# Expert rows turned by VectorE through HBM, thresholds in PSUM, and a shorter step of the search

## The chip, the cores and the metric

The kernel runs on one core of a Trainium2 chip. A core has five engines, each with its own instruction queue that it works through in order: TensorE (PE in the profile; PEld is its weight load), VectorE (DVE), ScalarE (ACT), GpSimd (POOL) and SyncE (SP, here only an issuer of DMAs). DMAs move data between HBM and the on-chip memory SBUF; PE writes its products to PSUM, which DVE and ACT read. The metric is the device time of one execution in microseconds, the median of several runs.

## The reference

Sigmoid attention over 8 batches of 12 heads, 448 positions and head width 64, and then a mixture of experts on its 3584 rows of 768:

```python
def _moe_ref(x, w_gate, w1, w2):
    N, D = x.shape; E = w_gate.shape[1]; cap = N // E          # 3584, 768; 8; 448
    flat = (x @ w_gate).flatten()
    for idx in np.argsort(-flat):                              # best logit first
        tok, e = idx // E, idx % E
        if assigned[tok] >= 0 or counts[e] >= cap: continue
        assigned[tok] = e; counts[e] += 1
    for e in range(E):
        mask = assigned == e
        out[mask] = np.maximum(x[mask] @ w1[e], 0.0) @ w2[e]   # F = 1024
```

Each expert gets exactly 448 rows, and which rows is settled one expert after the other: the expert that fills up first is found by a search for the threshold at which 448 rows count for it, its rows are taken out, and the next is searched.

## The kernel before, in words

**Attention first.** The first third of the span is attention; its result is written to HBM as `xs`, one row of 768 per token. Within a row the 32-wide pieces lie in an order that suits DVE's 32x32 transposes.

**Then eight experts, one after the other on PE.** Every matmul of an expert is done as three products of split operands (high x high, high x low, low x high), so that an expert takes 288 products: 144 with w1 (L858, L860, L862: four groups of 36) and 144 with w2 (L895, L897, L899: three groups of 48). The rows stand on the moving side as `xh` and `xl`, [128, 6, 448], the high and low part of the turned rows; the weights come as units of 18 or 24 products, loaded by SP (L703, L707), split into `wh` by ACT (L714) and `wl` by POOL (L716; for the last two experts every second one by DVE). After each w1 group ACT writes `hh` and `yt` (L866, L869) and POOL subtracts them to `hl` (L870). After each w2 group DVE turns the result (turn_y, L792), SP stores it to HBM and reads it back as rows, and POOL scatters these to the output (L814).

**Rows of the next expert.** While expert kx runs on PE, the rows of kx + 1 are prepared, once the router has listed them (L376 writes the list): four gathers by POOL (L736) for blocks of 128, 128, 128 and 64 rows; ACT puts each block's pieces in order (`order`, L745); PE transposes it in two trios of 128-wide transposes (`xturn`, L762); ACT writes xh from PSUM (L765) and DVE xl = p - xh (L766).

**The router** works meanwhile, mostly on DVE. Of search k: `keys` (L164 to L171), `ends` (two PE transposes, L180), then nine steps of `grid_search`, each three counts (L187) and a small sum (L192 to L242) on DVE alone; then `prove`: PE turns the eight thresholds and sums the counts (L291, L292), DVE makes from them `few`, `kr`, `km` (L295 to L302), reads one value for a branch (L304), and picks the expert (`choose`, L312 to L327). PE then sums the picked marks (`place`, L335, L340), DVE makes one-hot tables (L362), and PE turns these into the list (L367, L374). `bank()` gives out the router's two PSUM banks in turn.

**The order is written out by hand** in the loop at the end. Each product of PE adds 189 to `clock` (107 in the first, cut group of expert 0). When clock passes `t_route`, the router's next piece is issued at that place in all queues, and t_route is set to clock plus what the piece yields (the T_ numbers) plus SLACK = 150. Row work and scatters are `chores` with due times; at most one goes in 1000 of clock (CHORE_NS). While the rows of an expert are being turned by PE, `hold` pauses the router:

```python
if t >= t_route and (not hold["left"] or t < hold["from"]):
    t_route = t + next(route, 0) + SLACK
```

These numbers set only places in the order; an engine still waits for what an instruction needs.

Of the kernel before, what the change touches and what calls it, by code (L numbers as in the profile page):

```python
# [7 lines left out]
F32 = mybir.dt.float32  # L8
F32R = mybir.dt.float32r
# [4 lines left out]
AF = mybir.ActivationFunctionType  # L14
OP = mybir.AluOpType
# [13 lines left out]
LATE_PER_STEP = 1  # L29
LATE_KEYS = 3  # L30
T_KEYS, T_KE, T_STEP, T_DVE, T_KAP, T_PICK, T_TOT, T_OH, T_BT = 3600, 2100, 2050, 2025, 500, 2600, 600, 3800, 600
T_GRID, T_PROVE, T_FOUND = (0, 2290, 2480, 2480, 2480, 2480, 2480), 3000, 9000
T_LATER = 1000
SLACK = 150
CHORE_NS = 1000
# [3 lines left out]
W_DVE = 84  # L39
Y_WAIT, Y_LATE = 5000, 26000  # L40
N_FIRST, N_FAST = 3, 9
PAD = 176
NONE = 1.0e30
FOUND = 0x43E00000
ORDER = 2500
HOLD_NS = 1000


class Consts:
# [7 lines left out]

def route_consts(nc, cp, K):

    K.G = cp.tile([128, 128], BF, name="c_G")  # L60
    ti = cp.tile([128, 128], I32, name="c_ti")
# [5 lines left out]
    nc.gpsimd.iota(t9, [[0, 1]], base=0, channel_multiplier=1)  # L67
    K.CN = cp.tile([128, 32], F32, name="c_CN")
    nc.gpsimd.memset(K.CN, 0.0)
# [61 lines left out]
class Router:  # L131
# [156 lines left out]
    def prove(self, k):  # L288
        nc, K, wk = self.nc, self.K, self.wk
        p = self.bank()  # L290
        nc.tensor.transpose(p[:, :128], self.base.to_broadcast([128, 128]), K.ident)  # L291
        nc.tensor.matmul(p[:, 128:256], self.cnt.to_broadcast([128, 128]), K.G, start=True, stop=True)  # L292
        tr, cr = (p[:, o:o + 128].rearrange("p (e c) -> p e c", c=16)[:, :, 0] for o in (0, 128))
        few, kr = wk.tile([128, 8], F32, name="r_few"), wk.tile([128, 8], F32, name="r_kr")
        nc.vector.tensor_scalar(few, cr, 447.5, NONE, OP.is_lt, OP.mult)  # L295
        nc.vector.tensor_tensor(kr, tr, few, OP.subtract)
        km = self.km = wk.tile([128, 1], F32, name="r_km")
        nc.vector.tensor_reduce(km, kr, AX.X, OP.max)
        nc.vector.tensor_tensor(few, cr, few, OP.add)
        nc.vector.scalar_tensor_tensor(few, kr, km, few, OP.is_equal, OP.mult)  # L300
        ok = wk.tile([128, 1], F32, name="r_ok")
        nc.vector.tensor_reduce(ok, few, AX.X, OP.add)  # L302
        found = nc.vector.value_load(ok[:1].bitcast(I32))
        with self.tc.If(found != FOUND, preferred_fallthrough_block=True, label=f"found{k}"):  # L304
            self.exact(kr)
            nc.vector.tensor_reduce(km, kr, AX.X, OP.max)
        self.choose(kr[:112], km[:112])
# [112 lines left out]
def moe_attention(tc, q, k, v, w_gate, w1, w2, out):  # L420
    nc = tc.nc
    B, H, S, D = q.shape
    DM = H * D
    E, _, F = w1.shape
    CP, NCH, NP, ND, NF = 112, S // 112, H // 2, DM // 128, F // 128
    G4 = 4
    PSUM = bass.MemoryType.PSUM
    with contextlib.ExitStack() as ctx:
        ctx.enter_context(tc.manual_schedule())
        cp = ctx.enter_context(tc.tile_pool(name="cp", bufs=1))  # L430
        rw = ctx.enter_context(tc.tile_pool(name="rw", bufs=2))
        dr = ctx.enter_context(tc.tile_pool(name="dr", bufs=1, space=bass.MemoryType.DRAM))
# [3 lines left out]
        ps_s = pctx.enter_context(tc.tile_pool(name="pa_s", bufs=3, space=PSUM))  # L436
        cp.tile([128, PAD], F32, name="pad")
        ld = actx.enter_context(tc.tile_pool(name="ld", bufs=2))
        wk = actx.enter_context(tc.tile_pool(name="wk", bufs=2))
        xa = actx.enter_context(tc.tile_pool(name="xa", bufs=1))  # L440

        xs = dr.tile([B * S, DM], F32, name="xs")
        ys = [dr.tile([S, DM], F32, name=f"ys{i}") for i in range(2)]
        K = Consts()
        K.ident = ident = cp.tile([128, 128], F32, name="ident")
        bias = cp.tile([128, 1], F32, name="bias")
# [115 lines left out]

        def scale():

            a = rw.tile([128, CP], F32, name="s_a", bufs=1)
            nc.vector.tensor_scalar(a.bitcast(I32), LE[:, 0].bitcast(I32), 0x7FFFFFFF, None, OP.bitwise_and)
            m = rw.tile([128, 2], F32, name="s_m", bufs=1)
            nc.vector.tensor_reduce(m[:, :1], a, AX.X, OP.max)
            yield
            p = ps_t.tile([128, 512], F32, name="tp")  # L570
            nc.tensor.transpose(p[:, :128], m[:, :1].to_broadcast([128, 128]), ident)
            nc.vector.tensor_reduce(m[:, 1:], p[:, :128], AX.X, OP.max)
            K.D = cp.tile([128, 1], F32, name="c_D")
            nc.vector.tensor_scalar(K.D.bitcast(I32), m[:, 1:].bitcast(I32), 0x7F800000, None, OP.bitwise_and)
            K.kw = cp.tile([128, N_FAST + 1, 3], F32, name="c_kw")
            nc.vector.tensor_scalar(K.kw, K.cw, K.D, None, OP.mult)
            K.base0 = cp.tile([128, 1], F32, name="c_base0")
            nc.vector.tensor_scalar(K.base0, K.D, -2.0, None, OP.mult)
            K.T0 = cp.tile([128, 3], F32, name="c_T0")
            nc.vector.tensor_scalar(K.T0, K.kw[:, 0], K.base0, None, OP.add)  # L580
            yield
# [31 lines left out]
        for i in range(NPR + 1):  # L613
# [26 lines left out]
            if old and old[1] == NP - 1:  # L640
                b = old[0]
# [42 lines left out]
        xp = ctx.enter_context(tc.tile_pool(name="xp", bufs=1))  # L684
# [40 lines left out]
                split_w(state["split"])  # L725
                state["split"] += 1

        xg, xq, XH = {}, {}, {}

        def blocks():  # L730
            for j in range(4):
                yield j, min(128, S - 128 * j)

        def gather(kx, j, n):
            t = xg[kx, j] = xp.tile([128, DM], F32, name="xr", bufs=XR_BUFS)
            nc.gpsimd.indirect_dma_start(out=t[:n], out_offset=None, in_=xs,  # L736
                                         in_offset=bass.IndirectOffsetOnAxis(ap=listed[kx][:n, j:j + 1], axis=0))

        def order(kx, j, n):

            xq[kx, j] = xp.tile([128, DM], F32, name="xq", bufs=2)
            to = xq[kx, j][:n].rearrange("p (r a j) -> p r a j", r=ND, j=32)
            of = xg[kx, j][:n].rearrange("p (a r j) -> p r a j", r=ND, j=32)
            if kx or j > 1:
                nc.scalar.copy(to, of)  # L745
            else:
                nc.scalar.copy(to[:, :3], of[:, :3])
                nc.vector.tensor_copy(to[:, 3:], of[:, 3:])
# [19 lines left out]
        scat, chores = [], []  # L768
# [152 lines left out]
        clock = [0.0]  # L921
# [23 lines left out]
        for kx in range(E):  # L945
            turned = kx + 1 == E
            start = clock[0]

            def prepare():
                t0 = clock[0]  # L950
                lag = max(ORDER + 5000, min(14000, start + 40000 - t0))
                for j, n in blocks():
                    if kx:
                        chores.append((t0 + 1500 * j, kx + 1, lambda j=j, n=n: gather(kx + 1, j, n)))
                    else:
                        gather(1, j, n)
                bl = list(blocks())
                hold.update({"from": t0 + lag - HOLD_NS, "left": 2 * len(bl)})

                def turn_x(j, n, hf):  # L960
                    xturn(kx + 1, j, n, hf, False)
                    hold["left"] -= 1
                chores.append((t0 + lag - ORDER, kx + 1, lambda: order(kx + 1, *bl[0])))
                for i, (j, n) in enumerate(bl):
                    def first(i=i, j=j, n=n):
                        turn_x(j, n, 0)
                        if i + 1 < len(bl):
                            order(kx + 1, *bl[i + 1])
                    chores.append((t0 + lag + 1500 * j, kx + 1, first))
                    chores.append((t0 + lag + 1500 * j, kx + 1, lambda j=j, n=n: turn_x(j, n, 1)))  # L970

            def flush(kx):
                for c in [c for c in chores if c[1] <= kx]:
                    chores.remove(c)
                    c[2]()

            for step, cost in enumerate(moe(kx)):
                clock[0] += cost
                t = clock[0]
                if kx == 0 and step == 35:  # L980
                    flush(0)
                if t >= t_route and (not hold["left"] or t < hold["from"]):
                    t_route = t + next(route, 0) + SLACK
                if not turned and kx + 1 in listed:
                    prepare()
                    turned = True
                if t >= t_chore:
                    c = next((c for c in chores if c[0] <= t), None)
                    if c:
                        chores.remove(c)  # L990
                        c[2]()
                        t_chore = t + CHORE_NS
            if not turned:
                while kx + 1 not in listed:
                    next(route)
                prepare()
            flush(kx + 1)
# [28 lines left out]
```

## Time and profile before

| | |
|---|---|
| median of 3 runs | 846.31 us (845.62 to 850.72) |
| the profiled execution | 850.65 us, span 848.9 us |
| mean granted clock | 0.975 |
| attention and first list | 0 to 309 us |
| experts 0 to 7 begin at | 309.1, 384.9, 450.2, 514.7, 579.9, 644.8, 716.7, 779.9 us |

In the rows that follow, a line of the order of time is: start in us, duration in us, engine, line, operation, output <- inputs, shapes, count, and in brackets the idle time before it with the instruction that ended it. Matmuls are pipelined, so that durations overlap and the distance of starts is what one costs. A line of groups is: line, engine, operation, names, shapes, count, then busy us in all and mean ns of one, then idle time before them with the releasers. A line of stretches is: from and to, length, busy us and count of PE, PEld, DVE, ACT and POOL, granted clock, DMA share, GB/s.

### The profile page before, as it was taken

What the parts mean: (1) busy time and instruction counts of PE and PEld (TensorE: products, weight loads), DVE (VectorE), ACT (ScalarE), POOL (GpSimd) and SP (SyncE); (2) the same over time, 40 slices, a digit from 0 to 9 for tenths busy, and PEclk for the clock granted to TensorE, in tenths of its full rate; (3) what the DMA queues carried; (4) which work ended last, traced back from release to release, by engine and by line L of the source; (5) the groups of instructions that cost most, each with busy time, mean ns of one, the idle gap of its engine ahead of it and who ended that gap; (6) DMA issues with size and microseconds to landing.
All of it is one profiled execution on the core that took longest, in us unless ns stands there. A gap on an engine that the chain in (4) does not pass through costs nothing. (4 is left out here: it accounts for less than half of the span.)

```text
span 848.9 us, 14982 instructions
## 1 busy us (share of the span) xinstructions
PE 800.0 (94%) x5150; PEld 616.0 (73%) x5150; DVE 502.6 (59%) x1426; ACT 409.7 (48%) x506; POOL 467.1 (55%) x446
## 2 busy tenths in 40 slices
PE   6999999999999259899999999999999998999996
PEld 3454544554544149889989999989889887889996
DVE  4677666667663768568568558568678563232150
ACT  6777777777775143333433433433433423541421
POOL 9744444444420035745865875874874883481661
PEclk9999999999999669999999999999999999999998
DMA  8887877777770262365566576575665664845733
GB/s 171 169 179 155 185 172 159 167 177 154 176 151 19 94 186 70 100 183 164 176 196 189 146 207 197 156 211 162 187 199 169 169 210 126 241 138 138 226 130 131
DMA packets 259705, 138.71 MB, mean 163 GB/s; under 512 B 187136, under 2 KB 248832, under 8 KB 259616
## 3 DMA queue, kind: packets, MB, share of 16 engines
q1 hardware_dynamic: 246880, 104.14, 48.1%
q0 software_dynamic: 10880, 33.28, 13.0%
q8 instruction: 41, 0.67, 0.3%
q10 hardware_dynamic: 1856, 0.23, 0.2%
q14 instruction: 48, 0.39, 0.2%
HBM read 105.02 MB, written 32.57 MB: 162 GB/s over the span
## 5 line engine op out<-in xcount | busy, mean ns | idle before, releaser
L716 POOL TENSOR_TENSOR wl<-wr,wh 128x768 fp32r<-128x768 f32 (+1 forms) x96 | 203.5, 2133 | 68.9 <-ACT wh L714 66.0
L504 ACT ACTIVATE at<-sc,bias 128x896 f32<-128x896 f32 x168 | 161.6, 1004 | 40.7 <-PE sc L514 23.3
L464 POOL DMA_DIRECT2D nkq<-in_q_dram x188 | 118.5, 643 | 113.3 <-DVE kqT L489 106.1
L895 PE MATMUL sc<-hh,wh 128*128 128x448 f32 (+2 forms) x400 | 148.5, 371 | 0.4 <-ACT yt L827 0.4
L897 PE MATMUL sc<-hl,wh 128*128 128x448 f32 (+2 forms) x400 | 146.6, 367 | 0.0
L899 PE MATMUL sc<-hh,wl 128*128 128x448 f32 (+2 forms) x400 | 146.6, 366 | 0.0
L714 ACT ACTIVATE wh<-wr 128x768 fp32r<-128x768 f32 (+1 forms) x112 | 101.7, 937 | 92.1 <-PE sc L897 67.6
L862 PE MATMUL sc<-xh,wl 128*128 128x448 f32 (+2 forms) x396 | 144.8, 366 | 0.0
L858 PE MATMUL sc<-xh,wh 128*128 128x448 f32 (+2 forms) x396 | 144.1, 364 | 0.2 <-ACT xh L765 0.2
L860 PE MATMUL sc<-xl,wh 128*128 128x448 f32 (+2 forms) x396 | 144.2, 364 | 0.0
L870 POOL TENSOR_TENSOR hl<-yt,hh 128x896 fp32r<-128x896 f32 x32 | 68.1, 2129 | 96.0 <-ACT yt L869 84.8
L538 PE MATMUL tp<-at,nv 128*64 128x448 f32 x576 | 118.8, 548 | 0.0
L866 ACT ACTIVATE hh<-sc 128x896 fp32r<-128x896 f32 x32 | 29.5, 921 | 142.1 <-PE sc L862 142.1
L498 DVE TENSOR_TENSOR kqL<-kqT,kqH 128x896 fp32r<-128x896 f32 (+1 forms) x49 | 52.5, 1073 | 56.6 <-ACT kqH L497 56.5
L895 PEld LDWEIGHTS sc<-hh,wh 128*128 128x128 f32 x400 | 78.3, 196 | 4.6 <-ACT yt L827 0.6
L897 PEld LDWEIGHTS sc<-hl,wh 128*128 128x128 f32 x400 | 78.3, 196 | 4.6 <-issue 0.9
L899 PEld LDWEIGHTS sc<-hh,wl 128*128 128x128 f32 x400 | 78.3, 196 | 3.8 <-issue 0.2
L860 PEld LDWEIGHTS sc<-xl,wh 128*128 128x128 f32 x396 | 75.6, 191 | 6.0 <-DVE xl L766 0.4
L538 PEld LDWEIGHTS tp<-at,nv 128*64 128x64 f32 x576 | 37.1, 136 | 59.1 <-issue 56.7
L858 PEld LDWEIGHTS sc<-xh,wh 128*128 128x128 f32 x396 | 75.7, 191 | 5.8 <-ACT xh L765 0.4
L862 PEld LDWEIGHTS sc<-xh,wl 128*128 128x128 f32 x396 | 75.6, 191 | 5.7
L736 POOL DMA_INDIRECT xr<-xs,r_idx x32 | 32.0, 1001 | 72.8 <-ACT wh L714 57.2
(187 smaller groups left out, 1115.7 us busy)
## 6 DMA issues: line engine op xcount, KB each, us to landing
wr<-in_moe_w_dram SPq DMA_DIRECT2D x64, 384.0 KB
wr<-in_moe_w_dram SPq DMA_DIRECT2D x48, 512.0 KB
nkq<-in_k_dram SPq DMA_DIRECT2D x192, 56.0 KB
nkq<-in_q_dram POOLq DMA_DIRECT2D x188, 56.0 KB, 2.9
ys<-yt SPq DMA_DIRECT2D x92, 112.0 KB
xs<-xz SPq DMA_DIRECT2D x28, 336.0 KB
nv<-in_v_dram SPq DMA_DIRECT2D x92, 96.0 KB
xr<-ys SPq DMA_DIRECT2D x21, 384.0 KB
```

The lines of the kernel that those rows point to most:

```text
L464: qn.dma_start(t[o:o + 32, n], rws[x])
L504: nc.scalar.activation(a, p[:, :, :S], AF.Sigmoid, bias=bias, scale=1 / math.sqrt(D))
L538: nc.tensor.matmul(p[j * 64:j * 64 + 64, :S], nat["v", b, g][:, h0 + j, c, :], AT[b, pr, c][:, j, :], start=(c == 0), stop=(c == 2 and pr ...
L714: nc.scalar.activation(hi, raw[u], AF.Copy)
L716: eng.tensor_tensor(lo, raw[u], hi.bitcast(F32), OP.subtract)
L858: nc.tensor.matmul(ph[:, f, lo:hi], wh[:, a, fs], xh[:, dd, lo:hi], start=st, stop=False)
L860: nc.tensor.matmul(ph[:, f, lo:hi], wh[:, a, fs], xl[:, dd, lo:hi], start=False, stop=False)
L862: nc.tensor.matmul(ph[:, f, lo:hi], wl[:, a, fs], xh[:, dd, lo:hi], start=False, stop=en)
L870: nc.gpsimd.tensor_tensor(h2, h0, h1.bitcast(F32), OP.subtract)
L895: nc.tensor.matmul(py[:, d2, :w], wh[:, a, dsl], h1, start=st, stop=False)
L897: nc.tensor.matmul(py[:, d2, :w], wh[:, a, dsl], h2, start=False, stop=False)
L899: nc.tensor.matmul(py[:, d2, :w], wl[:, a, dsl], h1, start=False, stop=(j == 1 and a == 3))
```

## The change

Four things are done together.

1. Rows of experts 5, 6 and 7 (X_DVE = 5) are turned by DVE: the four gathers come as one chore; SP writes each gathered block to an HBM buffer `xd` (put_rows) and reads it back in two parts, so laid out (get_blocks) that DVE's 32x32 transposes finish the turn. DVE writes the turned block over the gathered one, ACT copies it to xh and DVE subtracts to xl (xturn_dve). `hold` isn't set for these experts. The tile xq grows to two blocks, for which PAD shrinks and s_a takes a tile of r_KE's ring.
2. kr, the eight thresholds, stays in the PSUM bank of the proof.
3. The pauses between search steps become 2290 and 2200 in place of 2480.
4. T_PROVE goes from 3000 to 2800, T_FOUND from 9000 to 8400.

```diff
-T_GRID, T_PROVE, T_FOUND = (0, 2290, 2480, 2480, 2480, 2480, 2480), 3000, 9000
+T_GRID, T_PROVE, T_FOUND = (0, 2290, 2290, 2200, 2200, 2200, 2290), 2800, 8400
-PAD = 176
+PAD = 32
+X_DVE = 5
+X_AT, X_PUT, X_GET, X_TURN = 21000, 5500, 10700, 17500
...
-        few, kr = wk.tile([128, 8], F32, name="r_few"), wk.tile([128, 8], F32, name="r_kr")
+        few, kr = wk.tile([128, 8], F32, name="r_few"), p[:, 256:264]
...
+        xd = [dr.tile([S, DM], F32, name=f"xd{i}") for i in range(2)]
...
-            a = rw.tile([128, CP], F32, name="s_a", bufs=1)
+            a = rw.tile([128, 224], F32, name="r_KE")[:, :CP]
...
+        def put_rows(kx, j, n):
+            nc.sync.dma_start(xd[kx % 2][128 * j:128 * j + n], xg[kx, j][:n])
+
+        def get_blocks(kx, g):
+            z = xz[kx, g] = xp.tile([128, 2, DM], F32, name="xq", bufs=2).rearrange("p h (b c) -> p (h b) c", c=192)
+            nb = min(8, S // 32 - 8 * g)
+            v = xd[kx % 2][256 * g:256 * g + 32 * nb].rearrange("(b t) (a c) -> a t b c", t=32, a=4)
+            for a in range(4):
+                nc.sync.dma_start(z[32 * a:32 * a + 32, :nb], v[a])
+
+        def xturn_dve(kx, j, n):
+            if j == 0:
+                XH[kx] = (xp.tile([128, ND, S], F32R, name="xh", bufs=2),
+                          xp.tile([128, ND, S], F32R, name="xl", bufs=2))
+            xh, xl = (x[:, :, j * 128:j * 128 + n] for x in XH[kx])
+            x = xg[kx, j][:, :ND * n].rearrange("p (r t) -> p r t", r=ND)
+            nc.vector.transpose(x.rearrange("p r (b t) -> p b r t", t=32),
+                                xz[kx, j // 2][:, j % 2 * 4:j % 2 * 4 + n // 32].rearrange("p b (r i) -> p b r i", i=32))
+            nc.scalar.activation(xh, x, AF.Copy)
+            nc.vector.tensor_tensor(xl, x, xh.bitcast(F32), OP.subtract)
+
         def order(kx, j, n):
-            xq[kx, j] = xp.tile([128, DM], F32, name="xq", bufs=2)
+            if j % 2 == 0:
+                xq[kx] = xp.tile([128, 2, DM], F32, name="xq", bufs=2)
+            xq[kx, j] = xq[kx][:, j % 2]
...
             def prepare():
+                if kx + 1 >= X_DVE:
+                    t0 = max(clock[0], start + X_AT)
+                    todo = [(0, lambda: [gather(kx + 1, j, n) for j, n in blocks()])]
+                    todo += [(X_PUT + 1150 * j, lambda j=j, n=n: put_rows(kx + 1, j, n)) for j, n in blocks()]
+                    todo += [(X_GET + 2300 * g, lambda g=g: get_blocks(kx + 1, g)) for g in range(2)]
+                    todo += [(X_TURN + 1300 * j, lambda j=j, n=n: xturn_dve(kx + 1, j, n)) for j, n in blocks()]
+                    chores[:0] = [(t0 + t, kx + 1, f) for t, f in sorted(todo, key=lambda x: x[0])]
+                    return
```

More of the change, by code (lines that the diff above doesn't have):

```diff
@@ L726, in stream @@
                 state["split"] += 1
-        xg, xq, XH = {}, {}, {}
+        xg, xq, xz, XH = {}, {}, {}, {}
         def blocks():
```

## The prediction

> **What bounds the kernel now.** I read the page first, then the stretches between expert starts, then the order of time on PE, on DVE and on POOL.
>
> ```profile
> PE 800.0 (94%) x5150; PEld 616.0 (73%) x5150; DVE 502.6 (59%) x1426; ACT 409.7 (48%) x506; POOL 467.1 (55%) x446
> ...
> 579.90:644.80 64.90, 64.58 (x355) 58.34 (x354) 47.28 (x182) 25.23 (x34) 45.91 (x30) 1.00 0.62 183
> 644.80:716.70 71.90, 68.65 (x389) 60.27 (x388) 40.84 (x149) 25.23 (x34) 46.90 (x31) 0.98 0.58 167
> 716.70:779.90 63.20, 61.85 (x314) 57.01 (x313) 18.22 (x18) 25.30 (x35) 31.79 (x21) 1.00 0.61 186
> ```
>
> After a stretch come its length and the busy times of PE, PEld, DVE, ACT, POOL, then the granted clock. The three stretches are experts 4, 5 and 6. PE is busy nearly throughout, so what counts is what PE must do and where it stands. Expert 4 is the normal case (64.9 us). Expert 5 is 7 us longer at a clock of 0.98, and expert 6 is short of DVE work (18.2 us) because no search is left.
>
> ```profile
> 619.84 0.20 PE L374 MATMUL rt<-c_SEL,r_bt 128*64 128x4 f16 x2
> ...
> 636.46 0.37 PE L899 MATMUL sc<-hh,wl 128*128 128x448 f32 x1
> 636.67 0.49 PE L762 MATMUL tp<-ident,xq 128*128 128x128 f32 x3
> 636.91 0.46 PE L895 MATMUL sc<-hh,wh 128*128 128x448 f32 x1
> 637.21 0.36 PE L897 MATMUL sc<-hl,wh 128*128 128x448 f32 x1
> ...
> 639.78 0.37 PE L899 MATMUL sc<-hh,wl 128*128 128x448 f32 x1
> 640.08 0.40 PE L762 MATMUL tp<-ident,xq 64*128 64x64 f32 x3
> 640.41 0.48 PE L895 MATMUL sc<-hh,wh 128*128 128x448 f32 x1
> 640.73 0.37 PE L897 MATMUL sc<-hl,wh 128*128 128x448 f32 x1
> ...
> 645.20 0.36 PE L862 MATMUL sc<-xh,wl 128*128 128x448 f32 x1
> 659.18 0.37 PE L862 MATMUL sc<-xh,wl 128*128 128x448 f32 x1
> ```
>
> Between the last two rows lie 69 products, so a product takes 0.203 us. Three row transposes cost PE 637.21 - 636.46 less two products, 0.34 us; those of the short block cost 640.73 - 639.78 less two, 0.54 us.
>
> **What goes.** An expert has six trios of the first kind and two of the second: 6 x 0.34 + 2 x 0.54 = 3.1 us of PE, and they go for experts 5, 6 and 7. For 6 and 7 waits go with them:
>
> ```profile
> 700.07 0.37 PE L899 MATMUL sc<-hh,wl 128*128 128x448 f32 x1
> 702.63 0.55 PE L762 MATMUL tp<-ident,xq 128*128 128x128 f32 x3 [2.19 <-ACT xq L745]
> ...
> 703.90:707.30 3.40, 3.40 (x12) 2.69 (x10) 1.68 (x3) 1.39 (x3) 1.71 (x1) 0.51 0.42 109
> ...
> 734.76 0.55 PE L762 MATMUL tp<-ident,xq 128*128 128x128 f32 x3 [1.04 <-ACT xq L745]
> ...
> 351.61 0.37 PE L899 MATMUL sc<-hh,wl 128*128 128x448 f32 x1
> 354.25 0.19 PE L335 MATMUL rt<-c_ones,r_mk 112*64 112x1 bf16 x1 [2.28 <-DVE r_ei L327]
> ...
> 355.80:359.20 3.40, 3.40 (x10) 3.01 (x10) 2.91 (x8) 0.00 (x0) 1.02 (x1) 0.50 0.38 116
> ```
>
> Expert 6's rows arrive late: 2.2 us of wait at 702.63, which I round up to 3.1 for the trios behind it, and a stretch of 3.4 us at half clock. Ten products in 3.4 us (the last row) in place of 16.7 lose 1.4 us: 4.5 us for all of it. Expert 7's rows cost 1.0 us at 734.76, which I round up to 1.6 in the same way. Rows together: 3 x 3.1 + 4.5 + 1.6 = **15.4 us off**.
>
> The wait at 354.25 is that of search 1 for DVE. It has a cause that the change meets:
>
> ```profile
> 341.93 0.17 DVE L295 TENSOR_SCALAR r_few<-rt 128x8 f32<-128x8 f32 x1 [3.89 <-PE rt L292]
> 342.60 2.03 DVE L300 SCALAR_TENSOR_TENSOR r_few<-r_kr,r_km,r_few 128x8 f32<-128x8 f32 x1
> 349.96 2.25 DVE L312 SCALAR_TENSOR_TENSOR r_w<-r_kr,r_km,c_rank 112x8 f32<-112x8 f32 x1 [5.14 <-DVEq L304]
> ...
> 665.09 0.25 DVE L300 SCALAR_TENSOR_TENSOR r_few<-r_kr,r_km,r_few 128x8 f32<-128x8 f32 x1
> ...
> 812.94 7.91 DVE L716 TENSOR_TENSOR wl<-wr,wh 128x1024 fp32r<-128x1024 f32 x1 [5.93 <-ACT wh L714]
> 812.95 2.14 POOL L870 TENSOR_TENSOR hl<-yt,hh 128x896 fp32r<-128x896 f32 x1
> 815.04 4.73 POOL L716 TENSOR_TENSOR wl<-wr,wh 128x1024 fp32r<-128x1024 f32 x2
> ```
>
> L300 on eight columns takes 0.25 us or 2.03, and a DVE subtraction takes 7.91 us while POOL works through three of its own: a DVE instruction with its inputs in SBUF stands until POOL's is over. With kr in PSUM I take L300 and L312 at 0.25 each, 3.8 us less. From L295 to L335 DVE then needs 12.3 - 3.8 = 8.5 us; T_FOUND at 8400 leaves 46 products, 9.3 us (49 before). The wait of 2.3 us and its half clock (the last row above), 1.4, go: **3.7 off**. If kr in PSUM frees nothing, they stay.
>
> The Trainium skill ("SBUF — State Buffer", Who interferes with whom) states that a DVE instruction with two SBUF inputs and a GpSimd one that reads SBUF shut each other out for a whole instruction. The rows agree on the wait, though 7.91 outlasts three. It speaks for kr in PSUM and against the new row split (below).
>
> **What the search steps do.** A step in every 13 products in place of 14 (2290 + 150 and 2200 + 150 over 189 both round up to 13) and two shorter pauses bring each listing forward by 8 + 1 + 3 products. I walked through the written order: each product adds 189 (107 in the first, cut group), the router goes when its time is past, one chore in 1000. That walk puts the old index of expert 5 (L374) at product 183 of expert 4. The trace has it at 619.84, 39.9 us in, which is 183 products and 2.7 us for the router's small matmuls; so I trust the walk, and it puts the new one at product 142. PE's gain from that alone is nothing: products bound it. The cover is DVE's slack at the proof:
>
> ```profile
> 600.35 0.17 DVE L295 TENSOR_SCALAR r_few<-rt 128x8 f32<-128x8 f32 x1 [2.24 <-PE rt L292]
> ...
> 592.58 0.27 DVE L242 TENSOR_SCALAR r_base<-r_acc,c_kw,r_base 128x1 f32<-128x1 f32 x1
> 595.03 0.27 DVE L242 TENSOR_SCALAR r_base<-r_acc,c_kw,r_base 128x1 f32<-128x1 f32 x1
> ...
> 625.96 0.39 DVE L183 COPY r_KE<-rt 128x224 f32<-128x224 f32 x1 [0.30 <-issue]
> 628.39 0.45 DVE L187 TENSOR_SCALAR_CACHE_REDUCE r_junk<-r_KE,r_T 128x224 bf16<-128x224 f32 x1
> ```
>
> A step takes DVE 2.45 us; 13 products give it 2.64. From the last row turn to the proof there were 116 products and there will be 108, 1.6 us less out of a slack of 2.24. Searches 2 to 5 fit, barely.
>
> **Search 6 does not fit.** Rows turned by PE pause the router through `hold`; the new branch of prepare() returns before that. So search 6 runs from product 169 of expert 4 (ends) to product 273 (step 8), and the four row turns fall between its steps at 235, 242, 249 and 256, in DVE's one queue:
>
> ```profile
> L601 DVE STREAM_TRANSPOSE xz<-xt 128x896 f32<-128x896 f32 x21 | 23.1, 1102 | 0.0
> L498 DVE TENSOR_TENSOR kqL<-kqT,kqH 128x896 fp32r<-128x896 f32 x47 | 51.4, 1093 | 56.5 <-ACT kqH L497 56.5
> L714 ACT ACTIVATE wh<-wr 128x768 fp32r<-128x768 f32 x64 | 52.4, 844 | 48.6 <-PE sc L897 25.2 <-DMA wr<-in_moe_w_dram 19.4 <-POOL wl L716 2.4
> ```
>
> A turn is a transpose (1.10 x 768/896 = 0.94 us), the ACT copy (0.84) and the subtraction (0.94), each waiting for the one before and DVE idle through ACT's: 2.9 us with two handoffs, 1.6 for the short block, 10.3 in all. To the last subtraction DVE needs 2.9 (ends to the first count, by 625.96 and 628.39) + 7 steps x 2.45 + two y turns of 1.05 + 10.3 = 32.4 us. PE covers the 119 products to expert 5 in 24.2, and some 1.6 of a wait for POOL (below). Expert 5's first products need all of xh and xl: PE stands 32.4 - 25.8 = 6.6 us. Its proof of search 6 comes one product later, with two steps and a count still to do (5.4 us): 5.2 more. **About 11.8 us on**, and after it the clock: one to two stretches like those at 0.50, 1.4 us each; I take 2.0.
>
> The Trainium skill ("TensorE: Matmul & The Clock Gate", Part 1) has the clock halve after an idle window of about 3.4 us and return after a busy one. Here 2.6 us of waiting were enough (351.61 to 354.25). By the Trainium skill, too, one to two such windows follow.
>
> At experts 6 and 7 no search runs beside the turns (products 204 to 230), so 58 products, 11.8 us, are left before the rows are wanted. ACT loses four copies an expert and writes xh in four instructions in place of eight; it wasn't late there.
>
> **DMAs and POOL.** The four stores and eight loads of an expert go through SP, and wait there for gathers and stores; weight loads stand behind them. They are asked for three units ahead (11 to 15 us), and the rows have 10 us from store to turn, so I take nothing; bounds 0 and 4 us. The wider xq, PAD and the shared r_KE ring add no instruction. Gathers in a row hold POOL:
>
> ```profile
> 612.10 2.14 POOL L870 TENSOR_TENSOR hl<-yt,hh 128x896 fp32r<-128x896 f32 x1
> ...
> 714.48 0.97 POOL L736 DMA_INDIRECT xr<-xs,r_idx  x1 [0.16 <-issue]
> 718.26 1.42 POOL L736 DMA_INDIRECT xr<-xs,r_idx  x1 [0.30 <-issue]
> ```
>
> Four take 5.2 us from 714.48 on. In expert 4 they come at product 144, ahead of the fourth hl: that ends at 614.2 + 5.2 = 619.4, and PE asks for it at product 174, at 579.9 + 35.3 + 2.6 of router work = 617.8: 1.6 us late. In experts 5 and 6 they come at product 112 and I take 2 and 1.4 by the same count: **5 on**, between 0 and 8. Earlier listings also put expert 3's gathers behind scatters: 1 on, between 0 and 2.
>
> **Sum**, against the profiled execution (850.65 us, span 848.9, 4.3 above the median of 846.31): -15.4 - 3.7 + 11.8 + 2.0 + 5 + 1 = +0.7, or 851. I carry the difference to the median: **847 us, no change**. A measurement of this kernel tells about 1% from none, 8.5 us.
>
> **Rivals.** *Faster*: the pile-up at expert 5 stays below some 4 us, since it is the difference of 32 and 26 us and ACT's handoffs or the first count may be shorter; gathers hidden too. For it: experts 6 and 7 gain whole. Against it: DVE's row turns have no other place in its queue. 847 - 8 - 1.4 of clock - 4 = 833.5; chance 0.27. *Slower*: the subtraction of the rows has both inputs in SBUF, where L766 read PSUM. If POOL holds it as at 812.94, two of the twelve standing 5 to 7 us add some 11 where nothing covers them, at expert 5: 858. It decides once POOL queues two operations when DVE arrives; for it the 7.91, against it the gaps that 45.9 us of POOL in a stretch of 64.9 leave. Chance 0.22. By the Trainium skill's page "SBUF — State Buffer" (Who interferes with whom) a held instruction waits for one POOL operation, up to 2.4 us each. *kr in PSUM frees nothing*: 851, within the forecast's band; a fifth of its chance. Forecast 0.51.
>
> The range runs from the fast rival to the slow one, 833 to 858. Faster by over 1%: 0.27; within: 0.51; slower: 0.22.
>
> **What would show it.** No L762 for experts 5 to 7; expert 5's first product waiting for DVE's xl by 4 to 9 us and L291 just behind it by 3 to 7, clock 0.5 after; no wait at L335 in expert 0; L300 and L312 near 0.25 us; expert 6 near 60 us. The prediction is wrong if expert 5 starts without a wait, if a weight load is late behind SP's row loads, or if the new subtractions take over 2 us.

## The result: slower by 3.4%, and the profile after

The changed kernel takes 876.35 us (median of 4 runs, 874.75 to 878.66) against 846.7 us for the kernel before on the same chip: a ratio of 1.0344 [1.0314, 1.0373], some 30 us. The prediction said 847 with a range up to 858. Its profiled execution has a span of 875.6 us. In the changed kernel the rows' lines are L739 (gather), L743 (put_rows), L751 (get_blocks), L760, L762, L763 (the turn), L790 (row turns on PE); products are L886, L888, L890 (w1) and L923, L925, L927 (w2); L717 and L719 make wh and wl.

The head of the page after, and its row of the DMA queue that carries loads:

```profile
span 875.6 us, 14869 instructions
...
PE 800.9 (91%) x5078; PEld 613.1 (70%) x5078; DVE 501.2 (57%) x1426; ACT 399.6 (46%) x482; POOL 468.4 (53%) x446
...
q1 hardware_dynamic: 254176, 112.40, 57.6%
```

The first thing to see is what did *not* change. PE was busy for 800.0 us and is busy for 800.9: the row transposes that went (3 x 3.1 us by the prediction) are made up, it seems, by a mean clock of 0.962 in place of 0.975, and the added time is idle time of PE. Second, queue q1 takes 57.6% of the DMA engines. Before:

```profile
q1 hardware_dynamic: 246880, 104.14, 48.1%
```

Over the span, q1 has 3% more packets, 8% more bytes and 24% more time for them (the share times the span). So packets got longer, and the stretches say where. Of each kernel the same 50 us of attention (length, busy us of PE, PEld, DVE, ACT, POOL, clock, DMA share, GB/s), first before, then after:

```profile
50.00:100.00 50.00, 49.91 (x438) 25.12 (x436) 34.30 (x65) 36.80 (x41) 22.63 (x36) 1.00 0.80 175
```

```profile
50.00:100.00 50.00, 49.91 (x442) 25.80 (x444) 34.66 (x71) 38.14 (x42) 22.97 (x38) 1.00 0.98 175
```

The same 175 GB/s cost 0.98 of the DMA engines in place of 0.80, in code that no part of the change was meant to touch. In the stretch from 0 to 50 us, where PE waits for inputs, this costs time (before, then after):

```profile
0.00:50.00 50.00, 42.75 (x296) 22.07 (x298) 28.53 (x42) 36.01 (x41) 40.48 (x80) 1.00 0.86 169
```

```profile
0.00:50.00 50.00, 38.20 (x242) 19.11 (x246) 23.03 (x30) 30.03 (x34) 36.75 (x74) 0.97 1.15 142
```

PE did 242 matmuls there where it had done 296. Expert 0 begins at 316.5 us in place of 309.1.

The rest lies in the experts. Experts 2, 4, 5 and 6 after, and PE's main waits (the order of time on PE, of which only rows that begin with a wait are shown):

```profile
456.00:525.10 69.10, 66.02 (x353) 59.04 (x353) 42.12 (x190) 25.00 (x35) 45.98 (x30) 0.98 0.61 172
...
591.50:663.30 71.80, 61.96 (x330) 55.99 (x328) 53.44 (x212) 20.44 (x25) 42.44 (x28) 0.97 0.72 204
663.30:738.00 74.70, 68.10 (x365) 59.89 (x366) 31.05 (x86) 23.07 (x28) 46.17 (x31) 0.91 0.63 180
738.00:806.00 68.00, 62.16 (x289) 56.44 (x288) 20.79 (x19) 21.85 (x26) 34.14 (x24) 0.95 0.76 215
```

```profile
507.71 0.55 PE L790 MATMUL tp<-ident,xq 128*128 128x128 f32 x3 [3.08 <-ACT xq L773]
...
632.35 0.48 PE L925 MATMUL sc<-hl,wh 128*128 128x448 f32 x1 [2.14 <-POOL hl L898]
...
663.30 0.74 PE L886 MATMUL sc<-xh,wh 128*128 128x448 f32 x1 [7.70 <-ACT xh L762]
...
668.66 0.48 PE L293 MATMUL rt<-ident,r_base 128*128 128x128 f32 x1 [4.62 <-DVE r_base L244]
...
712.86 0.48 PE L925 MATMUL sc<-hl,wh 128*128 128x448 f32 x1 [1.81 <-POOL hl L898]
...
776.08 0.48 PE L925 MATMUL sc<-hl,wh 128*128 128x448 f32 x1 [1.90 <-POOL hl L898]
...
792.04 0.58 PE L923 MATMUL sc<-hh,wh 128*128 128x448 f32 x1 [2.47 <-ACT wh L717]
...
794.47 0.74 PE L927 MATMUL sc<-hh,wl 128*128 128x448 f32 x1 [1.47 <-POOL wl L719]
```

Each row names the next culprit: late gathers in expert 2 (507.71), the pile-up on DVE at expert 5 (663.30 and 668.66), gathers ahead of `hl` in experts 4, 5 and 6, and late weights in expert 6 (792.04, 794.47).

### The profile page after: what moved, and what is told of

Its sections match the earlier page's. It is cut to its first block, busy times and chain, and to the rows that moved or that the text cites. A ratio compares the mean times of both kernels' runs of the same rounds, so it can differ in the third digit from the quotient of the medians.

```text
span 875.6 us, 14869 instructions
## 1 busy us (share of the span) xinstructions
PE 800.9 (91%) x5078; PEld 613.1 (70%) x5078; DVE 501.2 (57%) x1426; ACT 399.6 (46%) x482; POOL 468.4 (53%) x446
## 3 DMA queue, kind: packets, MB, share of 16 engines
q1 hardware_dynamic: 254176, 112.40, 57.6%
q0 software_dynamic: 10880, 33.28, 13.5%
## 4 chain that ended last, share of the span: by engine, by line
PE 36%; DMA 9%; issue 7%; POOL 7%; DVE 5%; ACT 1%; SPq 1%; POOLq 0%; DVEq 0%; ACTq 0%
PE sc L886 7%; PE sc L888 7%; PE sc L890 7%; PE sc L927 4%; POOL wl L719 4%; PE sc L923 4%; PE sc L925 4%; DMA xr<-xs,r_idx 4%; DMA wr<-in_moe_w_dram 3%; DMA xd<-xr 1%; PE tp L790 1%; POOL out_dram L842 1%; DVE r_junk L189 1%; POOL hl L898 1%; DVE r_oh L364 1%
## 5 line engine op out<-in xcount | busy, mean ns | idle before, releaser
L719 POOL TENSOR_TENSOR wl<-wr,wh 128x768 fp32r<-128x768 f32 (+1 forms) x96 | 206.7, 2168 | 90.4 <-ACT wh L717 90.1
L886 PE MATMUL sc<-xh,wh 128*128 128x448 f32 (+2 forms) x396 | 146.2, 369 | 7.9 <-ACT xh L762 7.7
L717 ACT ACTIVATE wh<-wr 128x768 fp32r<-128x768 f32 (+1 forms) x112 | 101.2, 935 | 113.7 <-DMA wr<-in_moe_w_dram 69.9
L925 PE MATMUL sc<-hl,wh 128*128 128x448 f32 (+2 forms) x400 | 146.4, 366 | 5.9 <-POOL hl L898 5.9
L927 PE MATMUL sc<-hh,wl 128*128 128x448 f32 (+2 forms) x400 | 148.5, 371 | 1.6 <-POOL wl L719 1.6
L923 PE MATMUL sc<-hh,wh 128*128 128x448 f32 (+2 forms) x400 | 146.9, 367 | 2.9 <-ACT wh L717 2.5
L888 PE MATMUL sc<-xl,wh 128*128 128x448 f32 (+2 forms) x396 | 145.9, 368 | 0.0
L890 PE MATMUL sc<-xh,wl 128*128 128x448 f32 (+2 forms) x396 | 145.2, 367 | 0.0
L886 PEld LDWEIGHTS sc<-xh,wh 128*128 128x128 f32 x396 | 75.9, 192 | 15.5 <-ACT xh L762 8.1
L925 PEld LDWEIGHTS sc<-hl,wh 128*128 128x128 f32 x400 | 78.9, 197 | 11.0 <-POOL hl L898 7.0
L923 PEld LDWEIGHTS sc<-hh,wh 128*128 128x128 f32 x400 | 78.9, 197 | 7.3 <-ACT wh L717 2.8
L927 PEld LDWEIGHTS sc<-hh,wl 128*128 128x128 f32 x400 | 78.9, 197 | 6.6 <-POOL wl L719 2.6
L888 PEld LDWEIGHTS sc<-xl,wh 128*128 128x128 f32 x396 | 75.9, 192 | 6.7 <-DVE xl L794 0.4
L890 PEld LDWEIGHTS sc<-xh,wl 128*128 128x128 f32 x396 | 75.9, 192 | 6.4
L517 PE MATMUL sc<-kqH 64*128 64x448 f32 x288 | 59.8, 412 | 10.5 <-ACT kqH L500 10.5
```

Source lines behind the costliest of these rows:

```text
L717: nc.scalar.activation(hi, raw[u], AF.Copy)
L719: eng.tensor_tensor(lo, raw[u], hi.bitcast(F32), OP.subtract)
L886: nc.tensor.matmul(ph[:, f, lo:hi], wh[:, a, fs], xh[:, dd, lo:hi], start=st, stop=False)
L888: nc.tensor.matmul(ph[:, f, lo:hi], wh[:, a, fs], xl[:, dd, lo:hi], start=False, stop=False)
L890: nc.tensor.matmul(ph[:, f, lo:hi], wl[:, a, fs], xh[:, dd, lo:hi], start=False, stop=en)
L923: nc.tensor.matmul(py[:, d2, :w], wh[:, a, dsl], h1, start=st, stop=False)
```

## The experiments

Twelve runs. The kernel before was timed beside each; its median was 848.2 to 848.5 us in all three sets. In what follows "PAD" is a filler tile: the tiles of attention are allocated behind it.

### Where the tiles lie: PAD alone, and PAD put right

The change makes three things ahead of attention's tiles smaller: PAD by 144 floats (576 bytes a partition), s_a, which moves into another ring (448), and the two buffers of r_kr (64). Attention's tiles begin 1088 bytes lower. The first run takes the kernel before and shrinks PAD alone (576 bytes); the second takes the changed kernel and gives 64 bytes back, so that the shift is 1024.

```diff
 # the kernel before
-PAD = 176
+PAD = 32
```

> The kernel before with PAD = 32 in place of 176 and nothing else: all SBUF tiles behind the pad stand 576 bytes lower, no instruction changes. Theory A (place in SBUF): the changed kernel's extra 7 us in the attention stage, where the changed code does not run, come from where the tiles stand (576 is 64 more than a multiple of 128), which makes short DMA packets slower; then this run is slower by 5 to 20 us (852 to 867), its attention stage ends some 7 us later, and the 256-byte packets average about 24 ns instead of 18. Theory B (place in HBM, or more traffic): the two new buffers xd are the cause; then this run is 846 as before.

```diff
 # the changed kernel
-PAD = 32
+PAD = 48
```

> The changed kernel with PAD = 48 in place of 32: tiles 64 bytes higher, which gives the attention pools the same place modulo 128 (and 512) as in the kernel before. Theory A: packets are fast again and the run comes near the sum of the prediction, 847 to 855, with the attention stage ending near 304 us in place of 311. Theory B: 876 as the changed kernel.

PAD alone makes the kernel before slower, 858.38 us, ratio 1.0121 [1.0089, 1.0154]. Sixteen floats of filler make the changed kernel faster, 867.01 us, 1.0209 [1.0183, 1.0234] against 1.0344. The stretch shown above, of the changed kernel with PAD 48:

```profile
50.00:100.00 50.00, 49.91 (x442) 25.41 (x438) 34.20 (x69) 37.14 (x40) 22.56 (x36) 1.00 0.79 172
```

The share is back at 0.79. Packet by packet (mean time in the records of the DMA engines, 100 to 150 us):

| packet | before | after | after, PAD 48 | before, PAD 32 |
|---|---|---|---|---|
| 128 bytes | 13 ns | 15 ns | 13 ns | 15 ns |
| 256 bytes | 18 ns | 25 ns | 18 ns | 25 ns |

Packets of 768 bytes, by their number the stores of xs out of SBUF, went the same way (50 to 100 us): 47 ns before, 57 after, 48 with PAD 48, 57 in the kernel before with PAD 32. So some 10 us of the 30 come from an edit that adds no instruction: short packets into and out of tiles that stand 64 bytes off. The shifts tried were 64, 576 and 1088 bytes (slow) and 0 and 1024 (not slow), 64 and 0 in the runs with kr in PSUM below; which multiple counts is not told apart by these.

### What is left: the pile-up at expert 5

With PAD 48 the lengths of the experts, from first product to first product (the last to the end of the span), against before:

| expert | 0 | 1 | 2 | 3 | 4 | 5 | 6 | 7 |
|---|---|---|---|---|---|---|---|---|
| before | 75.8 | 65.3 | 64.5 | 65.2 | 64.9 | 71.9 | 63.2 | 69.0 |
| after, PAD 48 | 73.3 | 66.6 | 68.9 | 66.0 | 71.8 | 74.4 | 68.1 | 68.9 |
| difference | -2.5 | +1.3 | +4.4 | +0.8 | +6.9 | +2.5 | +4.9 | -0.1 |

Two runs tested the pile-up: one stops the router (search 6) while DVE turns expert 5's rows, the other leaves expert 5's rows on PE.

```diff
+                    hold.update({"from": t0 + X_TURN - HOLD_NS, "left": 4})
...
-todo += [(X_TURN + 1300 * j, lambda j=j, n=n: xturn_dve(kx + 1, j, n)) for j, n in blocks()]
+todo += [(X_TURN + 1300 * j, lambda j=j, n=n: turn(j, n)) for j, n in blocks()]   # xturn_dve, then hold["left"] -= 1
```

> As the run with PAD = 48, and the router paused through hold from 1000 ahead of the first row turn by VectorE to the last one, as rows turned by TensorE pause it. Theory C (search 6 and the row turns of expert 5 fight for VectorE, 11.8 us and a half clock): 10 to 14 us faster than the PAD = 48 run, and expert 5's first product waits 0 to 3 us in place of 8, the proof behind it not at all. Rival D (what holds expert 5's first product is the rows' way through HBM, with late loads): at most 4 us faster than the PAD = 48 run.

```diff
-X_DVE = 5
+X_DVE = 6
```

> As the run with PAD = 48, but X_DVE = 6: expert 5's rows are turned by TensorE as before. Theory C: 8 to 13 us faster than the PAD = 48 run (the pile-up goes, 3.1 us of transposes come back, one gather in a row less on the list). Rival D: within 4 us of it. If also theory A holds, the run is near 836 to 842 and beats the kernel before.

Stopping the router gave 864.31 us, 1.0183 [1.016, 1.0207]: 2.7 us better, far less than expected. PE's waits with it:

```profile
651.99 0.74 PE L886 MATMUL sc<-xh,wh 128*128 128x448 f32 x1 [3.18 <-ACT xh L762]
...
663.24 0.32 PE L293 MATMUL rt<-ident,r_base 128*128 128x128 f32 x1 [3.07 <-DVE r_base L244]
```

Both waits shrank and neither went: search 6 now comes later and PE waits for its proof all the same. In neither of the two orders tried does DVE get through its work in time. Leaving expert 5 on PE gave 852.98 us, 1.0059 [1.0042, 1.0076], 14.0 us better; expert 4 is back at 64.6 us and PE has no gap at expert 5's start. That shows DVE's turn of expert 5's rows as one cause, at 14 us, a little above what had been expected. The price is that of all that goes with these rows: the two waits and their half clock, the gathers ahead of `hl` in expert 4 (a wait of 2.1 us) and the rows' DMAs, less the 3.1 us of transposes that come back.

### kr in PSUM alone, the search numbers alone

```diff
 # the kernel before
-few, kr = wk.tile([128, 8], F32, name="r_few"), wk.tile([128, 8], F32, name="r_kr")
+few, kr = wk.tile([128, 8], F32, name="r_few"), p[:, 256:264]
```

> The kernel before with kr kept in the PSUM bank of the proof and nothing else (one SBUF tile of the ring goes, so tiles behind it may move by 64 bytes). The theory of the prediction: L300 and L312 fall to about 0.25 us, the wait at L335 in expert 0 (2.3 us and a half clock) goes, 3 to 4 us faster. Rival: kr in PSUM frees nothing, within 1 us of before. If the packets of 256 bytes are long again (24 ns), the place of the tiles has moved, and the attention stage must be taken out of the comparison.

```diff
 # the kernel before
-T_GRID, T_PROVE, T_FOUND = (0, 2290, 2480, 2480, 2480, 2480, 2480), 3000, 9000
+T_GRID, T_PROVE, T_FOUND = (0, 2290, 2290, 2200, 2200, 2200, 2290), 2800, 8400
```

> The kernel before with the four numbers of the search alone changed (steps every 13 products, shorter pauses). The prediction's step: nothing from it but 1 us from expert 3's gathers behind scatters, so 847 to 850 against 848.5. Theory E (earlier listings cost what the changed kernel lost in experts 1 to 3, 6.5 us by the starts of its experts): 3 to 7 us slower, with a wait of about 3 us at a row turn in expert 2.

kr alone gave 853.91 us, 1.0073 [1.0046, 1.0101]: slower, since leaving out r_kr moves the tiles by 64 bytes and the packets are long again (the DMA share of 50 to 100 us is 1.01). Expert 0 is nevertheless 72.8 us in place of 75.8. So a run with PAD put right was needed:

```diff
 # the kernel before, kr in PSUM
-PAD = 176
+PAD = 192
```

> The kernel before with kr in PSUM and PAD = 192, which gives back the 64 bytes that the missing kr tile moved the attention pools by. If the place of the tiles alone made the kr run slow (theory A): packets of 256 bytes at 18 ns again, attention ending near 304 us, and the 3.0 us that expert 0 gained there stay: 844 to 846 against 848.4, faster than the kernel before by 2 to 4 us. If kr in PSUM has another cost: 849 or more.

It gave 845.92 us, 0.9961 [0.9939, 0.9982], the one version that beat the kernel before, by 0.4%. Packets of 256 bytes take 18 ns again, where kr alone had 24. Its L300 (instances, min/median/max ns, first and last start), and that of before:

```profile
L300 DVE SCALAR_TENSOR_TENSOR r_few<-rt,r_km,r_few x7: 224/225/227, 289.1 to 664.6; 128x8 f32<-128x8 f32 x7
```

```profile
L300 DVE SCALAR_TENSOR_TENSOR r_few<-r_kr,r_km,r_few x7: 229/444/2107, 288.6 to 665.1; 128x8 f32<-128x8 f32 x7
```

With one operand in PSUM the instruction takes 224 to 227 ns in all seven searches; with three operands in SBUF it took up to 2107.

The four search numbers alone cost 6.5 us: 854.86, 1.009 [1.0066, 1.0114]. Two of PE's waits in that run:

```profile
354.77 0.19 PE L335 MATMUL rt<-c_ones,r_mk 112*64 112x1 bf16 x1 [3.07 <-DVE r_ei L327]
...
501.39 0.55 PE L762 MATMUL tp<-ident,xq 128*128 128x128 f32 x3 [1.83 <-ACT xq L745]
```

The first is the wait that kr in PSUM takes away; the second, late rows in expert 2, is the one that stands at 507.71 in the changed kernel.

### The rows of experts 6 and 7: SP's queue

With X_DVE = 6, expert 6 was still 67.2 us where before had 63.2. Where SP stood in the changed kernel (its waits: us in all, times, longest), and its queue in expert 5:

```profile
SPq L743 <- DMA xr<-xs,r_idx: 48.4, 12, 13.5
```

```profile
692.11 0.37 SPq L710 DMA_DIRECT2D wr<-in_moe_w_dram  x1
705.97 0.34 SPq L743 DMA_DIRECT2D xd<-xr  x1
706.57 0.37 SPq L710 DMA_DIRECT2D wr<-in_moe_w_dram  x1
```

SP takes the store of the first block, whose gather hasn't landed, and stands 13.5 us; the weight load behind it goes out at 706.57. ACT sees it (its waits, and two of them in its order of time):

```profile
ACT wh L717 <- DMA wr<-in_moe_w_dram: 69.9, 12, 17.8
```

```profile
714.24 1.06 ACT L717 ACTIVATE wh<-wr 128x1024 fp32r<-128x1024 f32 x1 [6.79 <-DMA wr<-in_moe_w_dram]
...
790.93 1.06 ACT L717 ACTIVATE wh<-wr 128x1024 fp32r<-128x1024 f32 x1 [10.07 <-DMA wr<-in_moe_w_dram]
```

Before, ACT waited 19.4 us in all for weights, 17.6 of them once at the start; after, 69.9. The wait of 10.07 us is the one that PE meets at 792.04. Two runs moved the stores 6 us later, with everything behind them, the second with the gathers apart again:

```diff
 # after, PAD 48, X_DVE 6
-X_AT, X_PUT, X_GET, X_TURN = 21000, 5500, 10700, 17500
+X_AT, X_PUT, X_GET, X_TURN = 21000, 11500, 17500, 24500
```

> PAD = 48, X_DVE = 6, and the rows' stores 6000 later (X_PUT 11500), loads and turns 6800 and 7000 later. Theory F (SP stands in front of put_rows until the gathers have landed, 12 us at its longest, and the weight loads behind it come late: the 8 us that expert 6 lost against the prediction): SP's wait at put_rows falls from 17 us to under 5, PE's waits for wh and wl in expert 6 (2.4 and 1.9 us) go, 4 to 8 us faster than the run with X_DVE = 6 (853), so 845 to 849. Rival G (the memory traffic itself is what makes loads late): the same waits stay, within 2 us of 853.

```diff
 # the run above
-todo = [(0, lambda: [gather(kx + 1, j, n) for j, n in blocks()])]
+todo = [(1500 * j, lambda j=j, n=n: gather(kx + 1, j, n)) for j, n in blocks()]
```

> As the run before it, and the four gathers of an expert 1500 apart in place of one chore. The prediction's step (gathers in a row hold POOL 5.2 us, so that the fourth hl comes 2 us late in each expert): the two waits of 2.4 us at unit 9 of experts 5 and 6 go, 3 to 5 us faster than with gathers in a row. Rival: POOL is short anyway, waits stay, within 1.5 us.

They gave 855.54 us, 1.0082 [1.006, 1.0104], and 856.39, 1.0092 [1.0072, 1.0112]: no better than 852.98. SP's wait has to be read with care here. The sums of the view are, with X_DVE = 6 and then with late stores:

```profile
SPq L743 <- DMA xr<-xs,r_idx: 17.3, 5, 12.1
```

```profile
SPq L743 <- DMA xr<-xs,r_idx: 19.2, 7, 5.6
```

They leave out three of the eight stores in the first run and one in the second. In SP's order of time, with X_DVE = 6, SP issues nothing between 670.10 and the first store of expert 6's rows:

```profile
660.41 9.69 SPq L710 DMA_DIRECT2D wr<-in_moe_w_dram  x4
683.67 2.21 SPq L743 DMA_DIRECT2D xd<-xr  x2
```

Counted so over all eight stores, SP stood 32.8 us ahead of them, and 19.5 with late stores (longest 13.6 and 5.7). The waits of PE for wh and wl in expert 6 (2.07 and 1.32 us) went with it, as expected; but PE now stands for the rows at the start of experts 6 and 7:

```profile
716.03 0.51 PE L886 MATMUL sc<-xh,wh 128*128 128x448 f32 x1 [2.13 <-ACT xh L762]
...
783.11 0.47 PE L886 MATMUL sc<-xh,wh 128*128 128x448 f32 x1 [1.82 <-ACT xh L762]
```

With the gathers apart the first of these is 4.52 us. That run also tests what gathers in a row cost: in expert 5, where an `hl` now goes between the second gather and the third, PE's wait for it (2.00 us) is gone; in expert 6 POOL still works through the four gathers without a break, and the wait stays (2.86 and 2.85 us).

The last set asks the same of expert 7 alone, with the old search numbers: X_DVE = 7; the same with late stores; and the same with stores and loads of the rows issued by GpSimd.

```diff
 # after, PAD 48
-T_GRID, T_PROVE, T_FOUND = (0, 2290, 2290, 2200, 2200, 2200, 2290), 2800, 8400
+T_GRID, T_PROVE, T_FOUND = (0, 2290, 2480, 2480, 2480, 2480, 2480), 3000, 9000
-X_DVE = 5
+X_DVE = 7
```

> The changed kernel with PAD = 48, the old numbers of the search, and X_DVE = 7: only expert 7's rows go through HBM and VectorE, during expert 6, where no search runs. Theory H (row traffic and its waits stand in front of the weight loads in SP's queue): expert 6 takes 67 to 69 us in place of 63.2, as in the changed kernel, and the run is 3 to 6 us slower than the run with kr and PAD = 192. The prediction's step (a row turn without a search beside it saves 4.7 us and costs 1.4): 3 us faster than that run.

```diff
 # the run above
-X_AT, X_PUT, X_GET, X_TURN = 21000, 5500, 10700, 17500
+X_AT, X_PUT, X_GET, X_TURN = 21000, 11500, 17500, 24500
```

> As the run before it with stores 6000, loads 6800 and turns 7000 later; the pair of the next run. Theory H: the waits move from unit 10 towards the start of expert 7, time within 2 us of the run before it.

```diff
 # the run above
-            nc.sync.dma_start(xd[kx % 2][128 * j:128 * j + n], xg[kx, j][:n])
+            nc.gpsimd.dma_start(xd[kx % 2][128 * j:128 * j + n], xg[kx, j][:n])
...
-                nc.sync.dma_start(z[32 * a:32 * a + 32, :nb], v[a])
+                nc.gpsimd.dma_start(z[32 * a:32 * a + 32, :nb], v[a])
```

> As the run before it, but put_rows and get_blocks are issued by GpSimd, so that SP's queue carries neither them nor their waits. Theory H in its first form (SP's order): weight loads land in time again, ACT's waits for wr in expert 6 (9 us each with rows on SP) fall under 5, and the run is 3 to 6 us faster than the run before it. Rival (the DMA engines' time: eight loads of 768-byte packets take 5 us of all sixteen, whoever issues them): ACT's waits for wr stay, within 1.5 us. GpSimd's own cost: eight to twelve issues of 0.6 to 1 us, at a time when it stands idle.

| run | us | ratio | SP's wait at L743, us (longest) | ACT's wait for weights, us (times) | expert 6, us |
|---|---|---|---|---|---|
| X_DVE 7 | 850.92 | 1.0026 [1.0006, 1.0045] | 16.5 (11.5) | 45.2 (8) | 67.7 |
| stores late | 848.67 | 0.9994 [0.9968, 1.0019] | 6.7 (4.3) | 37.8 (6) | 63.7 |
| by GpSimd | 857.01 | 1.0098 [1.0066, 1.013] | (not on SP) | 18.3 (3) | 70.5 |

The first two rows ask it with one expert's rows alone. SP's wait fell, and with it went the waits of PE for weights; with X_DVE 7 these were

```profile
764.65 0.48 PE L923 MATMUL sc<-hh,wh 128*128 128x448 f32 x1 [2.39 <-ACT wh L717]
...
767.09 0.74 PE L927 MATMUL sc<-hh,wl 128*128 128x448 f32 x1 [1.75 <-POOL wl L719]
```

and expert 6 went from 67.7 to 63.7 us (in one profile each; the two intervals of the whole overlap a little). Part of these 4.0 us is the clock, 0.95 in expert 6 of the one and 1.00 in that of the other, and 1.4 us come back in expert 7 (71.0 in place of 69.6), at whose start PE now waits 1.37 us for rows and the clock halves. With the rows off SP's queue altogether, ACT's wait for weights is back to what it was before (17.6 of 18.3 us lie at the start): ACT's waits, and what PE waits for at expert 7's start:

```profile
ACT wh L717 <- DMA wr<-in_moe_w_dram: 18.3, 3, 17.6
```

```profile
783.47 0.74 PE L886 MATMUL sc<-xh,wh 128*128 128x448 f32 x1 [6.64 <-ACT xh L762]
```

Now the rows come late, since their DMAs stand among POOL's subtractions, and the run is 8.3 us slower where 3 to 6 us less had been expected. SP's rows above show a weight load held back by a store, and the same traffic on another queue leaves the weights in time: both point to the order of SP's queue as the cause of the late weights. One rival isn't excluded: the rows' DMAs also go out 7 to 8 us later in this run, so that they may no longer meet the same weight loads. That no version of rows through HBM beat the kernel before is measured; that none could is not.

The last set shows one thing more: with the old numbers, experts 1 to 3 of the changed kernel take 64.8, 64.5 and 64.8 us in place of 66.6, 68.9 and 66.0. Expert 2 of that run (X_DVE 7):

```profile
446.13:510.66 64.53, 64.53 (x355) 58.38 (x353) 41.72 (x182) 25.41 (x34) 46.77 (x31) 1.00 0.62 184
```

PE is busy for all 64.53 us. The shorter search numbers are what cost those three experts 7.4 us.

## Why the prediction was wrong, step by step

**The wider xq, PAD and s_a "add no instruction": the first failed step, +9 to 11 us.** They were counted at nothing because nothing is executed for them. They move attention's tiles by 1088 bytes, and 256-byte packets go from 18 to 25 ns. The row that would have warned was in the page of before: 246880 packets for 104.14 MB, a mean of 422 bytes, at a DMA share of 0.86 and 0.80 in the first two stretches of attention; a stage that lives on short packets at that share has little to give away. The Trainium skill ("DMA: Bandwidth & Descriptors", How a descriptor splits into AXI transactions) states that every transaction must start on a 256-byte boundary, so that a descriptor that starts off one costs more beats. By it, as an estimate, for tiles that stood on a boundary before and now start 64 bytes ahead of one, 256 bytes take 14 beats for 8 and 768 bytes 30 for 24. The trace agrees in direction, with 18 to 25 ns and 47 to 57; the rule is told of reads, the 256-byte packets write to SBUF, and what the absolute addresses are, no run here shows.

**Weight loads behind SP's row loads "at nothing": the second, the larger part of +8 in expert 6.** The step argued that loads are asked for 11 to 15 us ahead. SP stood up to 13.5 us for a gather: the cover was of the size of the wait. The bound of 4 us was given without a working, and the time that the queue stands for something not yet there is what it would have had to cover. Expert 6 was to gain 3.3 us and lost 4.9, with 4.0 us of waits for weights (2.71 and 1.32 with PAD 48) and 6.8 us at half clock behind them. It was named among what would make the prediction wrong.

**Earlier listings "behind scatters, 1 on": the third, +5.5.** Experts 1 to 3 lost 6.5 us with PAD 48, and 7.4 go when the old numbers return. The cover named was DVE's slack at the proof, and that held. The mechanism was named too; its size and reach failed. A list that comes earlier sends its gathers where POOL still has scatters and subtractions in front: the last three gathers of expert 3 were issued from 500.55 on, and PE waits at 507.71. With PAD 48 PE waited 1.17, 2.61 and 0.98 us for the rows of experts 2, 3 and 4, with 3.4 us at half clock at the second; with the old numbers 0.23, none and 0.24.

**The pile-up at expert 5: right, and its sizes close.** Predicted: a wait of 6.6 us at the first product, 5.2 at the proof of search 6, then half clock. Measured: 8.1 and 5.4 from start to start (7.70 and 4.62 by the rows), and

```profile
659.15:672.80 13.65, 4.86 (x13) 3.73 (x14) 9.97 (x41) 3.56 (x5) 5.34 (x3) 0.50 0.24 63
```

half clock for 13.65 us. A turn took 2.8 us where 2.9 was worked out; two of them in DVE's order (transposition, idle through ACT's copy, subtraction):

```profile
650.40 0.97 DVE L760 STREAM_TRANSPOSE xr<-xq 128x768 f32<-128x768 f32 x1
652.29 0.96 DVE L763 TENSOR_TENSOR xl<-xr,xh 128x768 fp32r<-128x768 f32 x1 [0.91 <-ACT xh L762]
653.16 1.11 DVE L820 STREAM_TRANSPOSE yt<-sc 128x896 f32<-128x896 f32 x1
654.19 0.94 DVE L760 STREAM_TRANSPOSE xr<-xq 128x768 f32<-128x768 f32 x1
656.04 0.96 DVE L763 TENSOR_TENSOR xl<-xr,xh 128x768 fp32r<-128x768 f32 x1 [0.91 <-ACT xh L762]
```

**Gathers in a row: right.** 1.6, 2 and 1.4 us predicted in experts 4, 5 and 6; the rows have 2.14, 1.81 and 1.90. That the gathers are what holds `hl` is shown for expert 5 alone, by the run with the gathers apart.

**kr in PSUM: right in mechanism.** L300 and L312 take 225 ns, and no product of expert 0 waits at L335's place any more. Expert 0 gained 2.5 us with PAD 48, 3.0 with kr alone and 1.2 with kr and PAD 192, where a wait for rows came instead (3.7 predicted). As a change by itself it is worth 2.3 us of the median (848.25 to 845.92).

**The rows' 15.4 us: 4.5 of them belong to one execution.** Expert 6's late rows (2.2 us and half clock at 702.63) were read from a profile 4.3 us above the median. Where the same code was profiled again, PE waited there 0.24 us (PAD 32), 0.36 (kr alone) and 2.41 (kr with PAD 192), and expert 5 took 68.2, 68.4 and 72.0 us in place of 71.9. To carry the whole difference to the median took off more than the usual execution holds; how much more, no run shows.

**The slower rival** (the rows' subtraction held by POOL) gave the right side for the wrong reason. Its twelve instructions, min/median/max ns:

```profile
L763 DVE TENSOR_TENSOR xl<-xr,xh x12: 558/958/2524, 652.3 to 803.0; 128x768 fp32r<-128x768 f32 x9, 128x384 fp32r<-128x384 f32 x3
```

One of the twelve took 2.5 us, none the 5 to 7 that the rival needed. (The faster rival's own sum gives 833.6, not 833.5.)

By terms of the sum, for PAD 48 against the kernel before: the terms summed to +0.7 and the run has +18.6; the misses are +8.2 in expert 6, +5.5 in experts 1 to 3, +1.7 and +0.9 in experts 4 and 5, +1.2 in expert 0, and 0.6 from a later end of attention (read from one profile each, so that they add up to within 0.2 us). The place of the tiles comes on top.

## What to carry to other kernels

An edit that only resizes a tile can move every tile allocated behind it: where a stage lives on DMA packets of 128 or 256 bytes, compare its DMA share and mean packet time first, before reading anything else. A DMA put on a queue that already carries loads is priced by how long the queue may stand for that DMA's input, against how far ahead the loads behind it are asked for. Bringing a producer forward is not free because its own engine has slack; follow what it releases into the next engine's queue. And a wait read from one profile is a term of that execution; before it is carried to the median, see whether a second profile has it.

## What the runs showed of the hardware

- Packets of 256 bytes from HBM into SBUF took 18 ns, and 24 to 25 ns when their tiles stood 64, 576 or 1088 bytes lower; 0 and 1024 left them at 18. GB/s stayed the same at a DMA share of 0.98 (175 and 175) and fell in the first 50 us, where the share came to 1.15 (169 to 142).
- A DVE instruction on three operands of eight columns took 229 to 2107 ns with all of them in SBUF and 224 to 227 with one in PSUM.
- At expert 5 PE stood twice (7.70 and 4.62 us), and its clock was at 0.50 for 13.65 us.
- The length of a wait doesn't decide alone whether the clock halves. With X_DVE 7 and late stores, 2.85 us up to 754.84 left it at 1.00 (first row); with the rows' DMAs on GpSimd, 2.85 us at the same product, up to 752.01, were followed by half clock (second row).

```profile
754.80:758.20 3.40, 3.37 (x16) 3.22 (x17) 0.00 (x0) 0.00 (x0) 3.23 (x3) 1.00 0.98 336
```

```profile
753.50:756.90 3.40, 3.40 (x11) 3.02 (x10) 0.00 (x0) 0.00 (x0) 2.94 (x6) 0.50 0.45 153
```
